# Linear attention, gated feed-forward and soft mixture of experts: the keys' maximum by 32x32 turns and partition swaps, and a new issue order

## Chip, cores and metric

One core of one Trainium2 chip. The metric is the device time of one execution in microseconds (us). TensorE (PE) multiplies, VectorE (DVE) and ScalarE (ACT) work element by element, GpSimd (POOL) does so too and issues part of the DMAs, SyncE (SP) issues the other DMAs.

## What is computed

The reference, cut to its core; all data is float32, with 8 batches, 8 heads, 576 positions and 64 features a head, so 4608 tokens of 512 features:

```python
q_s = softmax(q, axis=-1)                 # over the 64 features of a head
k_s = k - np.max(k, axis=2, keepdims=True)  # over the 576 positions
k_s = np.exp(k_s)
k_s = k_s / (np.sum(k_s, axis=2, keepdims=True) + 1e-09)
kv = np.einsum('bhsd,bhse->bhde', k_s, v)
x = np.einsum('bhsd,bhde->bhse', q_s, kv) # -> 4608 x 512
h = silu(x @ w_gate) * (x @ w_val)        # 512 -> 1536, twice
x = h @ w_out                             # 1536 -> 512
# soft mixture of experts: logits = x @ phi (32 slots); softmax over tokens feeds
# 8 experts with 4 slots each (w1: 512x1024, relu, w2: 1024x512);
# softmax over slots mixes their outputs back into each token
```

The change is about the second line: the maximum of the keys over the positions, for each of the 128 feature columns of two heads.

## The kernel before

**Tiles.** The 4608 tokens are ten blocks (eight of 512, two of 256). Attention works by batch b and by head pair p (0 to 3): a tile `kn` holds the keys of one pair, 128 partitions of positions by 128 feature columns by 5 position tiles. The gated layer works by block n and by column group i (0 to 11) in steps `pair n i`: a gate half of 12 matmuls (PSUM tile g), a value half of 12 matmuls (PSUM tile v), then Silu on ACT (L602), the product on DVE (L604, into `hT`), and for later blocks a 32x32 turn on DVE (L615) or a store. Below, "a half" is one such row of 12 matmuls of 512 columns, and halves are numbered in the order in which PE takes them.

**Keys' maximum.** `k_max(b, p)` reduces the 5 position tiles on DVE (L320, into `kpart`), turns the 128x128 result on PE (L323, `kpT`, into PSUM), and reduces it to one maximum a feature column (L326, `kmax`). `k_exp(b, p)` turns the maximum, spread over 128 columns, back on PE (L331, `kmbp`), subtracts it from the keys on DVE (L334) and takes the exponential on ACT (L338). `kv(b, p)` then multiplies with the values on PE (L346), and DVE and ACT norm the result (L352 to L355). For 8 batches of 4 pairs that is 64 turns on PE.

**Queries.** From block 2 on, `q_a` and `q_b` find maximum and sum of the queries with DVE reductions (L386, L422), four POOL copies between partition quarters (`swap`, L363), and one more DVE step (L390, L426); POOL subtracts and multiplies (L368); `q_tr` turns 32x32 blocks on DVE (L438). `x_mul` forms x on PE (L485, `px`), and ACT and DVE split it into a high and a low part (L495, L497).

**Weights.** The twelve weights W0 to W11 of the gated layer come as 64-bit numbers. Steps `w` load, `wa` (ACT, L518 and L520), `wb` (DVE, L525, L528, L532) and `wc` (POOL, L540) turn them into float32, `wh` (ACT, L553) and `wl` (DVE, L557) split them. The gate half of `pair 0 i` needs W i whole, that is after `wl i`.

**Order.** Nothing is scheduled by the compiler. The text `PROGRAM` lists steps; each mention of a step issues its next piece (up to the next `yield`), and each engine executes its instructions in that order. `@step` makes a POOL instruction wait until the named step's last DVE instruction is done. Loads of `kn`, `vn` and queries come from SP for batches 0 and 1 and from POOL after that.

**Memory.** PSUM tiles of tag m (three) are shared by `kpT`, `kmbp`, `px`, `kv` and others; g and v have two each. `kpart` has one buffer, `qst` four.

**End.** After `x 9 1`, the last step of the attention, POOL issues the loads of the expert weights (`piece`, L818), and the experts run as these land.

Of the kernel before, what the change touches and what calls it, by code (L numbers as in the profile page):

```python
# [39 lines left out]
def rows(n):  # L40
# [14 lines left out]
    vn 0 3, vn 0 2, kexp 0 3, kv 0 1, kexp 0 3, wb 3, kexp 0 2, kv 0 1, wb 3, qt 0 3, kexp 0 2, vn 0 0, w 1, kn 1 0,
    qa 1 0, wc 0@wb 3, wa 3 5, kv 0 1, kv 0 3, kv 0 0, kexp 0 2, qb 1 0, qb 0 2, kv 0 2, kv 0 0, kv 0 0, kv 0 3, wb 2,
    w 8, wa 1 3, w 4, kv 0 2, qb 1 0, qb 0 2@qa 1 0, qt 0 2, qt 0 2, x 0 0, wh 0, kv 0 3, q 1 1, kv 0 2, x 0 0, wb 2,
    wb 2, x 0 1, wl 0 v, x 0 0, x 0 0, x 0 0, kn 1 1, x 0 1, x 0 1, x 0 1, x 0 1, wb 3, qa 1 1, w 6, wc 2, wa 4 2,
    wh 2, pair 0 0, kmax 1 0, wl 2 v, wa 1 3, wc 3@qa 1 1, wb 1, pair 0 0, qb 1 0, wb 4, qb 1 1, kmax 1 0, qt 1 0,
    wh 3, const rep, wb 1, pair 0 0, wb 1, wl 3 v, w 5, wa 6 4, wc 1@wl 3 v, wa 4 2, pair 0 0, wb 4, q 1 2, pair 0 2,  # L60
    pair 0 2, kmax 1 0, qb 1 1, wh 1, wb 6, wl 1 v, pair 0 2, kmax 1 1, const rep, pair 0 3, pair 0 3, kmax 1 1, wb 6,
    vn 1 1, wb 4, w 7, wc 4@wl 1 v, pair 0 1, qb 1 1, qa 1 2, kmax 1 1, wa 5 3, kexp 1 0, qt 1 0, pair 0 2, wa 6 4,
    pair 0 3, kexp 1 1, wb 6, wc 6@wb 6, wa 7 5, wb 7, wh 4, wa 7 5, wl 4 v, kexp 1 0, wb 5, pair 0 1, pair 0 1, wh 6,
    pair 0 1, wb 5, pair 0 4, pair 0 4, kexp 1 1, wl 6 v, wa 5 3, vn 1 0, kexp 1 0, kv 1 0, wb 7, qb 1 2, kexp 1 1,
    kv 1 1, w 9 0, pair 0 3, qt 1 1, pair 0 6, wa 8 4, pair 0 6, wb 7, wa 8 4, wb 5, kv 1 1, wc 5@wb 5, qt 1 1, wb 8,
    pair 0 4, kv 1 0, wh 5, kv 1 0, pair 0 6, wb 8, wc 7@wb 8, wb 8, kn 1 2, wh 7, kmax 1 2, kmax 1 2, wl 5 v, kn 1 3,
    qb 1 2, q 1 3, pair 0 4, pair 0 3, qb 1 2, pair 0 2, wl 7 v, wa 9 5, wa 9 5, wc 8@wl 7 v, vn 1 2, vn 1 3,
    pair 0 5, pair 0 5, pair 0 5, kmax 1 3, wb 9, kmax 1 3, kv 1 1, pair 0 0, wb 9, pair 0 7, pair 0 6, kmax 1 3,
    wh 8, qa 1 3, kmax 1 2, qb 1 3, kexp 1 3, wb 9, kexp 1 3, wc 9@wb 9, w 10 1, kexp 1 2, kexp 1 2, pair 0 7, wl 8 v,
    kexp 1 3, kv 1 3, kexp 1 2, kv 1 3, wh 9, pair 0 7, kv 1 2, kv 1 2, kv 1 3, qt 1 2, wa 10 4, wl 9 v, pair 0 5,  # L70
    kv 1 2, w 11 0, wa 11 5, pair 0 8, qb 1 3, pair 0 6, wb 10, wb 10, wb 11, x 1 0, wb 10, pair 0 9, x 1 0, kn 2 0,
    wb 11, kn 2 1, q 2 1, vn 2 0, kmax 2 0, pair 0 8, pair 0 7, pair 0 7, wb 11, wa 10 4, qb 1 3, wc 10@wl 9 v, wh 10,
    pair 0 9, x 1 0, x 1 0, const phi, pair 0 8, x 1 0, o 1, wl 10 v, pair 0 8, x 1 1, qt 1 2, wa 11 5, qt 1 3,
    qt 1 3, x 1 1, x 1 1, x 1 1, x 1 1, pair 0 9, wc 11@wb 11, wh 11, wl 11 v, pair 0 10, pair 0 9, x 1 2, kmax 2 0,
    kmax 2 0, x 1 2, oa 1, pair 0 10, q 2 3, x 1 2, pair 0 11, x 1 3, pair 0 10, pair 0 10, ob 1, qa 2 1, x 1 2,
    x 1 2, qa 2 1@wl 11 v, qa 2 1, x 1 3, x 1 3, x 1 3, o 0, x 1 3, kexp 2 0, pair 0 4, oa 0, qa 2 1@qa 2 1, qb 2 1,
    qb 2 1, ob 0, pair 0 9, pair 0 11, pair 0 8, ob 1, pair 1 2, pair 1 2, ob 1, qb 2 1, oa 1, qa 2 3, pair 0 11,
    pair 1 2, kexp 2 0, kmax 2 1, pair 0 11, pair 1 2, qa 2 3, oc 1@ob 0, pair 1 4, pair 1 4, ob 0, pair 1 1,
    pair 0 10, pair 1 1, oa 0, qa 2 3, ob 0, oc 0@qa 2 3, kexp 2 0, kmax 2 1, o 2, op 0, pair 1 1, kmax 2 1, pair 1 1,
    pair 1 4, kv 2 0, op 1, op 0, qa 2 3, vn 2 1, qb 2 3, o 3, qb 2 1, oa 2, pair 1 2, qb 2 1@qb 2 1, kexp 2 1, ob 2,  # L80
    pair 1 3, oa 3, pair 1 3, qt 2 1, kn 2 3, ob 3, pair 0 1, pair 1 0, pair 1 3, pair 1 3, ob 2, pair 1 4, pair 1 0,
    pair 1 0, kexp 2 1, kv 2 0, pair 0 11, kmax 2 3, kv 2 0, ob 2, op 0, kexp 2 1, ob 3, qb 2 3, q 2 0, qa 2 0, op 1,
    kmax 2 3, pair 1 9, pair 1 1, qa 2 0, oa 3, pair 1 9, kmax 2 3, pair 1 9, qa 2 0, kv 2 1, oa 2, oc 2@qa 2 0,
    qa 2 0, pair 1 0, vn 2 2, op 0, pair 0 5, qb 2 0, qb 2 3, pair 1 9, kexp 2 3, kv 2 1, qb 2 0, pair 1 6, qb 2 0,
    pair 1 5, pair 1 5, ob 3, kn 2 2, pair 1 5, pair 1 11, qb 2 0, kexp 2 3, qb 2 0@qb 2 0, qt 2 0, pair 1 5,
    pair 1 11, q 2 2, qa 2 2, kmax 2 2, kmax 2 2, kv 2 1, kmax 2 2, pair 1 11, pair 1 11, oc 3@ob 3, qa 2 2, qa 2 2,
    x 2 0, x 2 0, kexp 2 2, kexp 2 2, pair 1 4, qa 2 2@qa 2 2, qb 2 2, qb 2 2, qb 2 2, o 5, pair 1 7, qb 2 3,
    pair 1 7, x 2 0, x 2 0, qb 2 3@qb 2 3, pair 1 6, kexp 2 3, qb 2 2, qt 2 3, pair 1 11, pair 1 7, pair 1 7,
    kexp 2 2, pair 1 7, x 2 0, pair 1 10, qb 2 2@qb 2 2, pair 1 6, kv 2 2, qt 2 2, pair 1 6, vn 2 3, q 3 0, kv 2 2,
    pair 1 0, kv 2 3, op 3, q 3 1, kv 2 3, kn 3 0, qa 3 1, vn 3 0, kv 2 2, op 1, op 1, pair 1 10, pair 1 10, qa 3 1,  # L90
    qa 3 0, qa 3 1, oa 5, kv 2 3, x 2 1, x 2 1, pair 1 10, pair 1 8, x 2 1, ob 5, op 2, x 2 1, qa 3 0, qa 3 0, x 2 1,
    vn 3 2, ob 5, pair 1 8, pair 1 8, kn 3 2, qa 3 0@qa 3 1, o 4, oa 4, oa 4, qb 3 0, pair 1 8, qb 3 0, qb 3 0@ob 5,
    pair 1 8, ob 4, ob 4, pair 2 0, pair 2 0, pair 1 5, pair 2 0, pair 2 0, op 2, qa 3 1, qb 3 1, pair 2 3, pair 2 3,
    pair 2 3, kmax 3 2, qb 3 1, pair 2 2, ob 4, oc 4, u 0, ua 0, ob 5, qb 3 1@ob 5, ub 0, pair 2 3, qb 3 0, qb 3 0,
# [1092 lines left out]
```

## Time and profile before

| | |
|---|---|
| median of 3 runs | 828.41 us (827.28 to 828.41) |
| the profiled execution, whole time | 831.53 us |
| its span | 829.8 us |
| PE busy | 781.6 us of the span |
| DVE, ACT, POOL busy | 481.7, 398.8, 261.7 us |

All rows come from one profiled execution, whose whole time is 831.53 us: 1.7 us more than its span and 3.1 us more than the median. "Busy" counts an engine's instructions; a matmul's end is modelled, so the time that a matmul takes from the next one is read from the starts of neighbours, not from its length. "Idle before" is the time in which an engine had nothing to do ahead of an instruction, with the instruction on another engine, or the DMA, that ended it.

### The profile page before, as it was taken

The numbers are of one execution on the slowest core, as the hardware profiler recorded it, in microseconds if no ns is written. First come the engines' busy times: TensorE is split into PE (matmuls) and PEld (weight loads), VectorE is DVE, ScalarE is ACT, GpSimd is POOL, SyncE is SP. The second block draws the span as 40 slices with busy tenths as digits, with TensorE's granted clock in tenths as the row PEclk, the third lists the DMA queues.
The fourth block names the chain that finished last, engine by engine and source line by source line (L and its number), as shares of the span: only waits on it lengthen the run. The fifth ranks groups of instructions, "written<-read, shape, count | busy, mean of one in ns | idle before, by whom it ended". The sixth has DMA issues, their size and how long they took to land.

```text
span 829.8 us, 15642 instructions
## 1 busy us (share of the span) xinstructions
PE 781.6 (94%) x6013; PEld 603.9 (73%) x6013; DVE 481.7 (58%) x1016; ACT 398.8 (48%) x636; POOL 261.7 (32%) x505
## 2 busy tenths in 40 slices
PE   3788999999999999999999999999999999998982
PEld 2666878877877786778777777786777788996640
DVE  7999864546565755567465666655544677144132
ACT  5978874556163562655452534333545264143032
POOL 3434343534442322322132134203132234333400
PEclk9999999999999999999999999999999999999996
DMA  9745446154245566565535573646343346999979
GB/s 359 289 147 166 149 157 211 58 212 148 100 121 151 154 148 167 128 167 160 146 80 143 141 198 76 168 140 190 92 87 100 77 117 212 297 355 398 406 286 385
DMA packets 103242, 151.08 MB, mean 182 GB/s; under 512 B 60032, under 2 KB 73728, under 8 KB 99200
## 3 DMA queue, kind: packets, MB, share of 16 engines
q1 hardware_dynamic: 86960, 90.19, 36.1%
q0 software_dynamic: 16208, 59.90, 21.1%
q8 instruction: 47, 0.77, 0.4%
q14 instruction: 27, 0.22, 0.1%
HBM read 105.22 MB, written 25.17 MB: 157 GB/s over the span
## 4 chain that ended last, share of the span: by engine, by line
PE 83%; DVE 6%; DMA 6%; ACT 2%; issue 1%; SPq 0%; POOL 0%; DVEq 0%; ACTq 0%; POOLq 0%
PE g L595 34%; PE v L595 33%; DMA piece<-in_w_dram 3%; PE lg L661 3%; PE dh L784 3%; PE px L485 2%; PE kv L346 2%; DVE W L557 1%; DMA qd<-in_qd_dram 1%; PE o L1060 1%; DMA f<-in_wgv_dram 1%; DVE ost L532 1%; DVE kn L334 1%; DVE ost L525 1%; PE qT L442 1%
## 5 line engine op out<-in xcount | busy, mean ns | idle before, releaser
L595 PE MATMUL g<-x,W 128*128 128x512 f32 (+1 forms) x1440 | 321.3, 374 | 5.5 <-DVE W L557 3.4
L595 PE MATMUL v<-x,W 128*128 128x512 f32 (+1 forms) x1440 | 316.3, 370 | 1.0 <-DVE hT L604 1.0
L595 PEld LDWEIGHTS g<-x,W 128*128 128x128 f32 x1440 | 251.8, 190 | 56.3 <-issue 4.4
L595 PEld LDWEIGHTS v<-x,W 128*128 128x128 f32 x1440 | 250.8, 189 | 50.0 <-issue 3.4
L604 DVE TENSOR_TENSOR hT<-hT,v 128x512 f32<-128x512 f32 (+1 forms) x120 | 74.6, 625 | 95.2 <-PE v L595 66.7
L602 ACT ACTIVATE hT<-g 128x512 f32<-128x512 f32 (+1 forms) x120 | 64.7, 554 | 132.5 <-PE g L595 111.7
L363 POOL COPY qsd<-qsd 32x16 f32<-32x16 f32 (+1 forms) x256 | 51.8, 202 | 195.6 <-DVE qsd L386 101.1
L368 POOL TENSOR_TENSOR qd<-qd,qsd 128x512 f32<-128x512 f32 (+1 forms) x64 | 59.9, 939 | 85.8 <-DVE qsd L390 40.1
L602 ACT ACT_TABLE_LOAD x56 | 71.8, 1283 | 22.2 <-PE g L595 7.2
L615 DVE STREAM_TRANSPOSE hB<-hT 128x512 f32<-128x512 f32 (+1 forms) x78 | 50.8, 671 | 1.0 <-DMA hN<-hB 0.2
L495 ACT ACTIVATE x<-px 128x512 fp32r<-128x512 f32 (+1 forms) x44 | 21.6, 516 | 46.5 <-PE px L485 34.2
L818 POOL DMA_DIRECT2D piece<-in_w_dram x54 | 28.5, 531 | 44.7 <-PE v L595 21.5
L334 DVE TENSOR_TENSOR kn<-kn,kmbp 128x640 f32<-128x640 f32 x32 | 25.7, 809 | 20.8 <-PE kmbp L331 20.8
L540 POOL TENSOR_TENSOR ost<-ost,f 128x1024 int32<-128x1024 int32 x9 | 23.2, 2581 | 40.9 <-DVE ost L532 11.0
L292 POOL DMA_DIRECT2D kn<-in_kn_dram x24 | 13.9, 578 | 68.2 <-PE kv L346 57.5
L338 ACT ACT_TABLE_LOAD x16 | 20.5, 1283 | 30.1 <-DVE kn L334 29.6
L338 ACT ACTIVATE kn<-kn 128x640 f32<-128x640 f32 x32 | 23.2, 736 | 23.2 <-DVE kn L334 23.1
L497 DVE TENSOR_TENSOR x<-px,x 128x512 fp32r<-128x512 f32 (+1 forms) x44 | 24.7, 577 | 13.3 <-ACT x L495 12.1
L326 DVE TENSOR_REDUCE kmax<-kpT 128x1 f32<-128x128 f32 x32 | 9.1, 285 | 40.0 <-PE kpT L323 39.9
L346 PEld LDWEIGHTS kv<-vn,kn 128*32 128x32 f32 x1280 | 23.8, 149 | 9.9 <-issue 3.8
L540 POOL TENSOR_TENSOR ost<-ost 128x1024 int32<-128x1024 int32 x9 | 22.9, 2544 | 21.4 <-DVE ost L532 8.9
L320 DVE TENSOR_REDUCE kpart<-kn 128x128 f32<-128x640 f32 x32 | 25.8, 806 | 6.6 <-DMA kn<-in_kn_dram 6.5
(175 smaller groups left out, 883.4 us busy)
## 6 DMA issues: line engine op xcount, KB each, us to landing
piece<-in_w_dram POOLq DMA_DIRECT2D x54, 512.0 KB, 8.0
hN<-hB SPq DMA_DIRECT2D x400, 48.0 KB, 2.2
f<-in_wgv_dram SPq DMA_DIRECT2D x9, 1024.0 KB, 9.4
vn<-in_vn_dram POOLq DMA_DIRECT2D x24, 325.0 KB, 4.5
kn<-in_kn_dram POOLq DMA_DIRECT2D x24, 320.0 KB, 4.1
out_dram<-ob SPq DMA_DIRECT2D x7, 1024.0 KB, 9.9
hT_dr<-hT SPq DMA_DIRECT2D x24, 256.0 KB, 5.4
qd<-in_qd_dram POOLq DMA_DIRECT2D x24, 256.0 KB, 4.5
```

The lines of the kernel that those rows point to most:

```text
L320: nc.vector.tensor_reduce(out=part, in_=kn_t[b, p], axis=AX, op=ALU.max)
L334: nc.vector.tensor_tensor(out=t, in0=t, in1=mb.unsqueeze(2).to_broadcast([128, 128, ST]), op=ALU.subtract)
L338: nc.scalar.activation(out=t, in_=t, func=ACTF.Exp)
L346: nc.tensor.matmul(acc[r:r + 32, :], lhsT=ek[:, r:r + 32, i], rhs=vv[:, i, r // D, :], start=(i == 0), stop=(i == ST - 1), tile_position=( ...
L363: nc.gpsimd.tensor_copy(out=st[a:a + 32, o + 1], in_=st[b:b + 32, o])
L368: nc.gpsimd.tensor_tensor(out=a, in0=a, in1=s, op=op)
L540: nc.gpsimd.tensor_tensor(out=d, in0=d, in1=t[:, c, 0], op=ALU.add)
L595: nc.tensor.matmul(gv[j], lhsT=W[i][:, w, k, j, :], rhs=x[:, k, :], start=(k == 0 and w == 0 and x is xh), stop=(k == KT - 1 and w == 1),)
L602: nc.scalar.activation(out=s, in_=g, func=ACTF.Silu)
L604: nc.vector.tensor_tensor(out=s, in0=s, in1=v, op=ALU.mult)
L615: nc.vector.transpose(out=hB[n, i // w][:, :, i % w, :], in_=s.rearrange("p (b j) -> p b j", j=32))
L818: nc.gpsimd.dma_start(out=ap, in_=src)
```

## The change

For batches 1 to 7 the keys' maximum goes another way, for two head pairs at once. `k_part` (`kr`) does the first reduction as before, into one half of a tile. `k_all` (`km`) then does: a 32x32 turn in place on DVE (128x256), a reduction to 128x8 on DVE, four POOL copies that swap neighbouring partition quarters, a maximum on DVE, four POOL copies that swap halves, a maximum on DVE, and a 32x32 turn of the spread result into one PSUM tile (128x256), from which `k_exp` subtracts. Batch 0 keeps its PE turns. Some small tiles share buffers with others. The whole of `PROGRAM` is laid out anew; it has as many steps as before (2301).

```diff
+    def k_part(b, p):
+        if len(kpart.get(b, ())) == 0:
+            kpart[b] = [sm.tile([128, 2, 128], F32, tag="kpart", bufs=1, name="kpart")]
+        nc.vector.tensor_reduce(out=kpart[b][0][:, len(kpart[b]) - 1], in_=kn_t[b, p], axis=AX, op=ALU.max)
+        kpart[b].append(p)
+
+    def k_all(b, h):
+        part, *ps_ = kpart.pop(b)
+        t = part.rearrange("p j (b i) -> p (j b) i", i=32)
+        nc.vector.transpose(out=t, in_=t)
+        st = sm.tile([128, 2, H], F32, tag="qst", bufs=4, name="kst")
+        o = st[:, 0]
+        nc.vector.tensor_reduce(out=o, in_=t, axis=AX, op=ALU.max)
+        yield
+        for x in (1, 2):
+            swap(st, 0, x)
+            yield
+            nc.vector.tensor_tensor(out=o, in0=o, in1=st[:, 1], op=ALU.max)
+            yield
+        mb = misc((128, 2, 128), "kmb")
+        nc.vector.transpose(
+            out=mb.rearrange("p j (b i) -> p (j b) i", i=32), in_=o.unsqueeze(2).to_broadcast([128, 8, 32])
+        )
+        for j, p in enumerate(ps_):
+            kmax[b, p] = mb[:, j]
+
     def k_exp(b, p):
-        mx, mb = kmax.pop((b, p)), misc((128, 128), "kmbp")
-        nc.tensor.transpose(mb, mx.to_broadcast([128, 128]), ident)
-        yield
+        mb = kmax.pop((b, p))
+        if not b:
+            mx, mb = mb, misc((128, 128), "kmbp")
+            nc.tensor.transpose(mb, mx.to_broadcast([128, 128]), ident)
+            yield
         t = kn_t[b, p]
...
-    def swap(st, o):
+    def swap(st, o, x=1):
 
         for g in range(4):
-            a, b = 32 * g, 32 * (g ^ 1)
+            a, b = 32 * g, 32 * (g ^ x)
             nc.gpsimd.tensor_copy(out=st[a:a + 32, o + 1], in_=st[b:b + 32, o])
```

Four lines of the new order, from the stretch in which the weights W1 to W4 are made ready, and `kr` and `km` of batch 1 stand among them:

```diff
+    x 0 1, x 0 1, pair 0 0, wc 3@qa 1 1, wh 2, wl 2 v, wh 3, pair 0 0, wa 6 4, w 4, wb 1, wl 3 v, q 1 2, wb 6, kr 1 1,
+    kr 1 0, km 1 0, qb 1 1, wa 4 2, wb 4, vn 1 1, pair 0 0, vn 1 0, w 9 0, qt 1 0, wc 1@wl 3 v, qb 1 1, wh 1, wb 6,
+    wb 4, km 1 0, wb 4, w 7, km 1 0, pair 0 2, pair 0 2, pair 0 2, qb 1 1, w 8, wl 1 v, pair 0 3, wa 4 2, qt 1 1,
+    wb 6, pair 0 1, km 1 0, wc 4@wl 1 v, qa 1 2, wa 6 4, pair 0 1, qt 1 0, wc 6@wb 6, wa 5 3, kn 1 2, wa 7 5, km 1 0,
```

## Rows read from the trace of the kernel before

**Rows 1.** The page: span, and each engine's busy time.
```profile
span 829.8 us, 15642 instructions
PE 781.6 (94%) x6013; PEld 603.9 (73%) x6013; DVE 481.7 (58%) x1016; ACT 398.8 (48%) x636; POOL 261.7 (32%) x505
```

**Rows 2.** Three stretches: length, busy us (instructions) by engine, PE clock, DMA share, GB/s.
```profile
0.00:92.34 92.34, 69.16 (x620) 54.03 (x621) 83.49 (x120) 73.12 (x159) 34.87 (x23) 0.96 0.60 218
92.34:690.00 597.66, 594.09 (x4063) 460.08 (x4062) 350.33 (x757) 289.32 (x395) 187.78 (x414) 1.00 0.50 139
690.00:829.80 139.80, 118.32 (x1335) 89.83 (x1334) 47.85 (x141) 36.32 (x84) 39.03 (x70) 0.95 0.91 341
```

**Rows 3.** What PE waited for from 92.34 to 690: us, times, longest.
```profile
PE px L485 <- DVE wp L580: 2.1, 1, 2.1
PE v L595 <- DVE hT L604: 0.8, 1, 0.8
PE kv L346 <- ACT kn L338: 0.7, 3, 0.3
```

**Rows 4.** PE in order of time: start, length, instruction; turns alone between halves.
```profile
349.46 2.89 PE L595 MATMUL v<-x,W 128*128 128x512 f32 x12
352.19 0.27 PE L323 MATMUL kpT<-ident,kpart 128*128 128x128 f32 x1
352.21 3.00 PE L595 MATMUL g<-x,W 128*128 128x512 f32 x12
355.05 0.27 PE L331 MATMUL kmbp<-ident,kmax 128*128 128x128 f32 x1
355.07 3.01 PE L595 MATMUL v<-x,W 128*128 128x512 f32 x12
357.92 2.88 PE L595 MATMUL g<-x,W 128*128 128x512 f32 x12
360.64 0.62 PE L595 MATMUL v<-x,W 128*128 128x512 f32 x2
```

**Rows 5.** PE in order of time: turns beside other work between halves.
```profile
167.99 0.27 PE L323 MATMUL kpT<-ident,kpart 128*128 128x128 f32 x1
168.19 1.09 PE L485 MATMUL px<-qsT,kvs 64*64 64x128 f32 x16
169.21 0.32 PE L331 MATMUL kmbp<-ident,kmax 128*128 128x128 f32 x1
169.29 3.00 PE L595 MATMUL g<-x,W 128*128 128x512 f32 x12
```

**Rows 6.** Groups by line and shape: busy us, mean ns of one, idle before.
```profile
L323 PE MATMUL kpT<-ident,kpart 128*128 128x128 f32 x32 | 9.8, 308 | 10.5 <-DMA ident<-in_ident_dram 6.6 <-DVE kpart L320 3.9
L326 DVE TENSOR_REDUCE kmax<-kpT 128x1 f32<-128x128 f32 x32 | 9.1, 285 | 40.0 <-PE kpT L323 39.9
L438 DVE STREAM_TRANSPOSE qsT<-qd 128x256 f32<-128x256 f32 x8 | 3.5, 442 | 3.8 <-POOL qd L368 2.9 <-PE px L485 0.9
L386 DVE TENSOR_REDUCE qsd<-qd 128x8 f32<-128x256 f32 x8 | 3.2, 396 | 2.5 <-DMA qd<-in_qe_dram 2.5
L390 DVE TENSOR_TENSOR qsd<-qsd 128x8 f32<-128x8 f32 x8 | 1.2, 145 | 0.3 <-POOL qsd L363 0.3
L363 POOL COPY qsd<-qsd 32x8 f32<-32x8 f32 x64 | 11.8, 185 | 44.8 <-DVE qsd L422 21.5 <-DVE qsd L386 21.3
```

**Rows 7.** What DVE waited for, whole span: us, times, longest.
```profile
DVE kn L334 <- PE kmbp L331: 20.8, 11, 3.4
DVE qsd L426 <- POOL qsd L363: 7.8, 10, 1.0
DVE qsd L390 <- POOL qsd L363: 5.3, 7, 2.2
```

**Rows 8.** PE in order of time, in the start; idle before it in brackets.
```profile
33.38 4.60 PE L595 MATMUL g<-x,W 128*128 128x512 f32 x12 [2.10 <-DVE x L497]
77.87 4.15 PE L595 MATMUL g<-x,W 128*128 128x512 f32 x10 [1.75 <-DVE W L557]
92.34 0.95 PE L595 MATMUL g<-x,W 128*128 128x512 f32 x3
```

**Rows 9.** DVE in order of time, in the start.
```profile
43.70 1.22 DVE L557 TENSOR_TENSOR W<-ost,W 128x1024 fp32r<-128x1024 f32 x1
44.83 0.68 DVE L604 TENSOR_TENSOR hT<-hT,v 128x512 f32<-128x512 f32 x1
45.43 2.57 DVE L528 TENSOR_SCALAR ost<-ost 128x1024 int32<-128x1024 int32 x1
...
89.24 1.74 DVE L557 TENSOR_TENSOR W<-ost,W 128x1024 fp32r<-128x1024 f32 x1
```

**Rows 10.** POOL in order of time, in the start.
```profile
44.99 2.45 POOL L540 TENSOR_TENSOR ost<-ost,f 128x1024 int32<-128x1024 int32 x1 [5.37 <-DVE W L557]
```

More of the change, by code (lines that the diff above doesn't have):

```diff
@@ L55 @@
[L55 to L94, printed above, removed]
@@ new lines @@
+    pair 0 6, km 1 1, wb 9, pair 0 7, wh 8, wb 9, qt 1 2, qa 1 3, vn 1 3, kv 1 1, km 1 1, const phi, km 1 1, wb 9,
+    km 1 1, kexp 1 3, pair 0 5, pair 0 5, kexp 1 2, q 2 1, wa 9 5, pair 0 7, kexp 1 3, pair 0 5, kv 1 3, wl 8 v,
+    kv 1 3, w 10 1, wc 9@wb 9, kexp 1 2, vn 2 0, pair 0 4, kv 1 2, kn 2 1, kv 1 2, qb 1 3, kv 1 2, wh 9, wl 9 v,
+    pair 0 6, wa 10 4, wb 10, wb 10, pair 0 8, kv 1 3, wa 10 4, qb 1 3, wb 10, pair 0 8, qa 2 1, x 1 0, pair 0 7,
+    pair 0 9, kn 2 0, pair 0 8, pair 0 8, x 1 0, pair 0 9, x 1 0, wc 10@wl 9 v, w 11 0, wa 11 5, wb 11, wb 11,
@@ new lines @@
+    qb 4 2, pb 2, qa 4 1, lt 0 0, ts 0 0, ts 0 0, ts 0 0, qb 4 1, ud 2, ts 0 0, pair 3 2, pair 3 2, pair 3 2,
+    pair 3 7, sh 2 2, sh 2 2, ts 0 0, pair 3 1, ts 0 0, kn 4 2, kr 4 2, pb 2, qb 4 2, pb 2, kv 4 3, kn 4 1, ts 0 0,
+    ts 0 0, pc 2, pair 3 1, qb 4 1, qb 4 1, lt 0 1, vn 4 1, pair 3 1, pair 3 2, qb 4 1, qb 4 1, qt 4 1, pair 3 0,
+    pair 3 1, pb 2, pb 2, q 4 3, vn 4 2, lg 3 0, kr 4 1, qb 4 2, pair 3 5, pair 3 10, pair 3 10, km 4 1, km 4 1,
+    km 4 1, pair 3 4, km 4 1, pair 3 10, qb 4 2, pair 3 4, pc 2, km 4 1, km 4 1, kv 4 3, kv 4 3, kexp 4 1, kn 5 1,
@@ new lines @@
+    kv 5 2, kv 5 2, kexp 5 3, sh 4 0, kv 5 3, kv 5 3, kv 5 2, q 6 0, kn 6 0, kn 6 1, kv 5 3, lg 4 1, x 5 1, x 5 1,
+    x 5 1, pair 4 11, pair 4 11, pair 4 11, pair 4 8, sh 4 1, sh 4 1, qa 6 0, kr 6 1, x 5 1, x 5 1, qa 6 0, qa 6 0,
+    pair 4 9, vn 6 1, qa 6 0, qb 6 0, pair 5 3, pair 5 1, pair 5 1, pair 4 8, pair 4 7, pair 4 11, kr 6 0, lt 1 0,
+    pair 5 3, pair 4 6, qa 6 1, qa 6 1, pair 5 2, qb 6 0, pair 4 9, qa 6 1, qa 6 1, qb 6 1, pair 5 3, qb 6 1,
+    pair 5 1, pair 4 10, lg 4 2, qb 6 0, lg 1 0, pair 4 11, km 6 0, sh 4 2, sh 4 2, pb 3, pair 4 9, pair 5 0,
@@ new lines @@
+    kv 7 1, x 7 0, km 7 1, pc 1, qb 7 3, km 7 1, qb 7 3, qt 7 3, q 8 1, pair 6 5, qb 7 2, pair 6 5, pair 6 11,
+    pair 6 11, pc 5, qb 7 2, x 7 0, vn 7 3, pair 6 9, pd 4, pair 6 9, pair 6 5, pair 6 11, x 7 0, km 7 1, qa 8 1,
+    qa 8 1, kexp 7 2, pair 6 4, qt 7 2, qa 8 1, kexp 7 3, kexp 7 3, pair 6 10, q 8 0, qa 8 1, qb 8 1, pair 6 10,
+    kexp 7 2, qb 8 1, pair 6 10, kv 7 2, kv 7 3, lg 6 1, kv 7 2, sh 6 0, sh 6 0, qb 8 1, kv 7 3, kv 7 2, kv 7 3,
+    x 7 1, sh 6 1, pair 6 10, qb 8 1, sh 6 1, pair 6 8, pair 6 8, sh 6 1, pair 6 6, x 7 0, x 7 1, pair 6 7, qb 8 1,
@@ L942, in exp_table @@
     def exp_table(_=0):
-        t = sm.tile([128, 1], F32, tag="one", name="one")
+        t = sm.tile([128, 1], F32, tag="krs", name="one")
         nc.scalar.activation(out=t, in_=ident[:, 0:1], func=ACTF.Exp)
     def u_rz():
-        rz = keep["rz"] = sm.tile([128, 1], F32, tag="rz", name="rz")
+        rz = keep["rz"] = sm.tile([128, 1], F32, tag="krs", name="rz")
         nc.vector.tensor_scalar_add(rz, Z, EPS)
```

288 lines of the change are left out of this document (153 added, 135 removed).

## The prediction

> **What bounds the kernel now.** I read the busy times first, then the three stretches, then what PE waits for. PE is busy for 781.6 of 829.8 us [rows 1], but the 48 us that it is idle are not spread evenly. In the middle stretch, 92.34 to 690 us, PE is busy for 594.1 of 597.7 us at full clock, with DVE at 59% and POOL at 31% [rows 2]. Its idle time of 3.6 us there is one wait of 2.1 us and four small ones [rows 3]. So the middle is bound by the sum of PE's work: what PE no longer does there comes off the time, unless a wait takes its place. In the start, 0 to 92.34, DVE is busy for 83.5 us and PE for only 69.2 [rows 2]: PE gets its halves as fast as DVE makes the weights ready. Twice a half comes after a wait on DVE and then runs slowly (4.60 us against a spacing of 2.7) [rows 4, 8]. In the end, from 690, the DMAs are 91% busy at 341 GB/s [rows 2]; the expert weights flow there, their loads begin after the last attention step, and the order from that step on is nearly the same text. An earlier middle moves the end forward as a whole, so I cost the end at nothing. If DMA bandwidth were taken by something moved into it, that cover would be gone; no load of keys, values or queries is left by then.
>
> **PE: the turns that go.** For batches 1 to 7, 28 head pairs lose two turns each, 56 of 64. Eight of these stand ahead of the half that first uses W8, where PE follows DVE; they are counted at nothing. 48 stand in the middle stretch. What one is worth is read from neighbouring starts. Two halves in a row start 2.72 us apart (357.92 to 360.64) [rows 4]. With a `kpT` between them, 352.19 to 355.05 is 2.86, so 0.14 us for the turn; with a `kmbp`, 355.05 to 357.92 is 2.87, so 0.15. Beside other work a turn at the head of a group holds the next step for 0.20 us (167.99 to 168.19), and one at its tail for 0.08 (169.21 to 169.29) [rows 5]. Counted in the old text, the 48 are 17 in groups of their own (9 alone, 4 times two) at 0.145, which makes 2.5 us, and 31 beside other work at 0.13, near the middle of 0.08 and 0.20, as heads and tails of groups are about equally many: 4.0. Sum 6.5 us; with all 31 at 0.08 or at 0.20 it is 5.0 or 8.7.
>
> The instruction itself is listed at 308 ns in the mean and 0.27 us in the middle stretch [rows 4, 6], most of it beside the next instruction; taken whole, 48 x 0.27 would be 13.0 us. The Trainium skill ("TensorE: Matmul & The Clock Gate", Part 4: PE-mode transpose) gives about 275 ns for a 128x128 turn in one kernel's context; by that figure 13.2 us would stand here instead of 6.5. The listed length agrees with the page, the spacing of the starts doesn't, and the sum goes by the spacing.
>
> **PE: the regrouping.** Counted in the two texts behind the first W8 half, the old order leaves the halves 60 times for other work, 13 of them for turns alone; that leaves 47, against 41 in the new order. A break costs about what a lone turn does, 0.13 us: 6 x 0.13 = 0.8 us, with bounds 0 and 1.5. Of ACT's table loads, the new text asks for 106 changes between Silu and Exp instead of 112, on an engine that is half idle [rows 1]: nothing.
>
> **DVE.** For each set of two pairs two reductions at 0.285 go (0.57 us). In come a turn of 128x256 (0.44), a reduction to 128x8 (0.40), two maxima (0.145 each) and a turn into PSUM, for which no row stands; its bounds are the 128x256 turn at 0.44 and twice that, and I take 0.44 [rows 6]. That is 1.57, so 1.0 us more a set and 14 us in all; DVE goes from 482 to about 496 us. Twelve sets lie in the middle, where DVE is idle for 247 us [rows 2]. It also loses its waits on PE's turns, 39.9 and 20.8 us [rows 6, 7]. On POOL 14 x 8 copies at 0.185 make 20.7 us, beside 410 idle us in the middle [rows 2, 6]. ACT keeps its work.
>
> **The added wait.** DVE now waits twice a set for four POOL copies. Behind it on DVE stand the products that free PE's value tile; PE has two of these, so a wait shorter than a pair (5.4 us) stays hidden. The same hop exists for the queries, 64 times, and cost DVE 7.8 + 5.3 us in 17 waits, at most 2.2 [rows 7]: about 0.2 a hop, 28 hops, 6 us of idle DVE. On POOL the copies stand among key loads and query steps, which come later by up to 0.74 a hop; with both in order, a load stuck on a busy buffer would hold DVE too. PSUM tiles of tag m are asked for 42 times less, which only loosens. For the waits of PE in the middle I keep today's 3.6 us, a change of 0, with bounds -3.6 (all go) and +7 (0.5 us a set).
>
> **The start.** Here the sets of batch 1 and the new order meet the engine that binds. I summed DVE's work by the rows' durations up to the last step that a weight needs. Up to `wl 5` both orders have 61.2 us; up to `wl 8` the old has 71.8 and the new 74.2: two sets (+2.0) and one more product (+0.7), less a cast moved. Now W8 is ready at 90.98 (89.24 + 1.74) and its half starts at 92.34 [rows 8, 9], so 1.4 of the 2.5 are covered and PE waits 1.1 us more. Against that stand the holds. When POOL runs a weight step of 2.45 us, a DVE instruction that comes beside it can be held to its end: 2.57 us at 45.43 where 0.68 is usual, until POOL's 44.99 + 2.45 [rows 9, 10]. POOL has nine weight steps (L540) before 92.34, of which one stands in the rows. In the new text `wc 1` runs beside `kr`, `kr` and the first turn of `km`, which may give the 1.9 us of this hold back. I take +1.1, with bounds -4 (two holds gone) and +12 (below). The loads of W0, W2, W3 and W1 keep their order on SP; those of W4 to W9 change places, behind DMAs that are 60% busy over the start [rows 2], and I cost them at nothing. If one came late, its W would wait by the time of a load.
>
> **Sum.** -6.5 - 0.8 + 0 + 1.1 = -6.2 us on the profiled 831.5, so 825.3 there. The profiled time stands 3.1 above the median of 828.4, so the forecast is 822.2 us.
>
> **Rivals.** (A) The whole length: if a turn costs PE its listed 0.27 us, 828.4 - 13.0 - 0.8 + 1.1 = 815.7. For it speaks the list, against it the spacing between halves. The page cited above would have it so. Chance 0.10.
>
> (B) The hop takes the gain: each of the 14 sets holds PE by 0.5 us, because in an order packed this tightly DVE's wait for POOL falls where a half waits for its tile: 822.2 + 7 = 829.2, no change. For it speaks that several `kv` steps follow closely on the set that feeds them (`kv 4 1` with no half between), against it that PE waited for keys' exponentials only 0.7 us in the whole middle [rows 3]. Chance 0.20.
>
> (C) Slower: the holds in the start. The two maxima of a set read two SBUF inputs, as the weight subtraction does that was held. If each of batch 1's four maxima comes beside a weight step of POOL and is held to its end, DVE is late by 4 x 2.4 = 9.6 us in the one stretch where it binds, and PE, idle longer, takes one more half at the slow rate (+1.9, 4.60 against 2.72) [rows 4, 8]: 822.2 + 9.6 + 1.9 = 833.7. It decides the sign once the start loses more than the 7.3 us that PE gains. For it speaks `wc 6`, issued right ahead of the second maximum of the first set; against it, that holds are there in the old order too, so only additional ones count. The Trainium skill ("GPSIMD Engine Reference", 8. Key points) says that POOL shares its SBUF interfaces with DVE, in contention with DVE instructions that have two SBUF inputs or a two-port mode; the held rows agree. Chance 0.18.
>
> (D) The turns beside other work were free, because PE lost that time to the change of shape anyway, so the change takes away less than it says: 2.5 + 0.8 off, 828.4 - 3.3 + 1.1 = 826.2. For it speaks that a half after a `px` or a turn is late by nearly the same [rows 5]. Chance 0.10, just faster.
>
> The forecast itself has 0.42. Faster by over 0.2% (under 826.8; 0.2% is about what a measurement of this kernel can tell from no change) collects 0.42 + 0.10 and most of (D): 0.60. Within 0.2%: 0.22, that is (B) and the rest of (D). Slower: 0.18. The range must leave out no more than 2 in 10: from 815, which takes in (A), to 831.5, which takes in (B) and the lighter half of (C). The forecast's own range is 818 to 826.
>
> **What would show it.** Right: PE has 56 instructions less (5957) and L323 and L331 stand at 8 turns in all; PE's idle time in the middle stays at 2 to 6 us while that stretch is 5 to 9 us shorter; the half that first uses W8 starts at 92 to 95 us; DVE stands near 496 us and POOL near 282. (A) would show as a middle shorter by 12 us or more; (B) as waits of PE for DVE behind the copies; (C) as held DVE instructions in the start and a W8 half after 100 us. The prediction fails if the new order moves work that I did not sum (ACT's table loads, query steps) in front of a half, or if the end starts later than the middle allows, which would show as the last attention step not moving forward with the halves.

## The result and the profile after

The changed kernel takes 816.02 us, the median of four runs (815.42 to 816.83), against 828.41 for the kernel before, measured beside it. The ratio is 0.9837, with a 95% interval of 0.9812 to 0.9862. The gain is 12.4 us, twice the forecast 6.2. The profiled execution of after took 816.83 us (span 815.1), 0.8 above its median, where that of before stood 3.1 above its own. So the two spans differ by 14.7 us, and that is the number that the stretches below have to add up to. In the later rounds of runs the kernel before had medians of 830.28 to 830.89 us (eight to ten runs each), so the 828.41 of this round stands low, and 12.4 is rather the lower end of the gain. In one kernel below (the new middle behind the old start) one execution of six took 1968.21 us; it is left out of that kernel's median and ratio.

The page of after, span and busy times (it answers to [rows 1]):

```profile
span 815.1 us, 15636 instructions
PE 771.2 (95%) x5957; PEld 594.6 (73%) x5957; DVE 481.0 (59%) x1058; ACT 390.2 (48%) x630; POOL 288.8 (35%) x617
```

PE lost 56 instructions and 10.4 us of busy time, and DVE's total did not rise. To see where the time went, the span is cut at two places that can be found in both kernels: the start of the 17th half, the first that needs W8 (92.34 us before [rows 8], 83.76 after), and the start of the 204th half. First the three stretches of after (columns as in [rows 2]):

```profile
0.00:83.76 83.76, 63.88 (x612) 50.93 (x612) 73.56 (x122) 69.30 (x148) 42.37 (x40) 0.98 0.65 248
83.76:673.15 589.39, 588.83 (x4015) 454.88 (x4009) 359.82 (x796) 280.76 (x397) 205.80 (x506) 1.00 0.51 140
673.15:815.10 141.95, 118.47 (x1339) 88.84 (x1337) 47.61 (x143) 40.10 (x88) 40.59 (x72) 0.95 0.89 336
```

Then the same two later stretches of before, from the same halves:

```profile
92.34:689.56 597.22, 593.65 (x4059) 459.64 (x4058) 349.89 (x756) 288.88 (x395) 187.35 (x413) 1.00 0.50 139
689.56:829.80 140.24, 118.76 (x1339) 90.27 (x1337) 48.29 (x142) 36.76 (x84) 39.46 (x70) 0.95 0.90 340
```

The start is 8.6 us shorter (92.34 to 83.76), the middle 7.8 (597.22 to 589.39), and the end 1.7 longer. In the middle PE's busy time fell by 4.8 us and its idle time by 3.0. What is left of the idle time is two waits. PE's waits in the middle of after (us in total, times, longest):

```profile
PE lrep L724 <- DVE llo L706: 0.4, 1, 0.4
PE v L622 <- DVE hT L631: 0.2, 1, 0.2
```

The new way itself, by groups (busy us, mean ns of one | idle before), in after:

```profile
L320 PE MATMUL kpT<-ident,kpart 128*128 128x128 f32 x4 | 1.9, 467 | 10.8 <-DMA ident<-in_ident_dram 6.5 <-DVE kpart L317 4.3
L390 POOL COPY kst<-kst 32x8 f32<-32x8 f32 x112 | 27.6, 247 | 62.2 <-DVE kst L340 45.5 <-DVE kst L345 12.2
L345 DVE TENSOR_TENSOR kst<-kst 128x8 f32<-128x8 f32 x28 | 5.9, 210 | 7.2 <-POOL kst L390 7.1
L348 DVE STREAM_TRANSPOSE kmb<-kst 128x256 f32<-128x256 f32 x14 | 6.3, 450 | 0.2
```

Only batch 0's four `kpT` are left. The turn into PSUM, for which no row stood, takes 450 ns (0.44 was taken). DVE waited 7.1 us for the copies in 28 hops, against the 6 expected. The copies took 27.6 us where 20.7 were taken. So the parts of the change cost what was forecast, or not much more; the difference lies elsewhere, above all in the start.

### The profile page after: what moved, and what is told of

Same layout as the page of the kernel before. It is cut to its first block, busy times and chain, and to the rows that moved or that the text cites. A ratio compares the mean times of both kernels' runs of the same rounds, so it can differ in the third digit from the quotient of the medians.

```text
span 815.1 us, 15636 instructions
## 1 busy us (share of the span) xinstructions
PE 771.2 (95%) x5957; PEld 594.6 (73%) x5957; DVE 481.0 (59%) x1058; ACT 390.2 (48%) x630; POOL 288.8 (35%) x617
## 4 chain that ended last, share of the span: by engine, by line
PE 85%; DMA 7%; DVE 4%; ACT 2%; issue 1%; SPq 0%; DVEq 0%; POOLq 0%
PE v L622 35%; PE g L622 34%; DMA piece<-in_w_dram 4%; PE dh L811 3%; PE kv L373 3%; PE lg L688 3%; PE px L512 2%; DMA vn<-in_vn_dram 1%; PE o L1087 1%; DMA h0T<-hT_dr 1%; DVE W L584 1%; DMA q<-in_q_dram 0%; PE hNp L668 0%; DVE ost L559 0%; PE h L1023 0%
## 5 line engine op out<-in xcount | busy, mean ns | idle before, releaser
L622 PE MATMUL g<-x,W 128*128 128x512 f32 (+1 forms) x1440 | 318.1, 372 | 1.3 <-DVE x L524 1.3
L395 POOL TENSOR_TENSOR qd<-qd,qsd 128x512 f32<-128x512 f32 (+1 forms) x64 | 61.6, 968 | 69.3 <-DVE qsd L454 32.5
L390 POOL COPY kst<-kst 32x8 f32<-32x8 f32 x112 | 27.6, 247 | 62.2 <-DVE kst L340 45.5
L449 DVE TENSOR_REDUCE qsd<-qd 128x16 f32<-128x512 f32 (+1 forms) x32 | 19.4, 607 | 17.4 <-ACT qd L446 17.3
L446 ACT ACTIVATE qd<-qd 128x512 f32<-128x512 f32 (+1 forms) x32 | 18.4, 577 | 23.5 <-POOL qd L395 23.3
L373 PE MATMUL kv<-vn,kn 128*32 128x65 f32 x1280 | 26.6, 238 | 2.9 <-ACT kn L365 1.9
L413 DVE TENSOR_REDUCE qsd<-qd 128x16 f32<-128x512 f32 (+1 forms) x32 | 19.3, 605 | 16.7 <-DMA qd<-in_qd_dram 8.5
```

The costliest lines, as they stand in the source:

```text
L373: nc.tensor.matmul(acc[r:r + 32, :], lhsT=ek[:, r:r + 32, i], rhs=vv[:, i, r // D, :], start=(i == 0), stop=(i == ST - 1), tile_position=( ...
L390: nc.gpsimd.tensor_copy(out=st[a:a + 32, o + 1], in_=st[b:b + 32, o])
L395: nc.gpsimd.tensor_tensor(out=a, in0=a, in1=s, op=op)
L622: nc.tensor.matmul(gv[j], lhsT=W[i][:, w, k, j, :], rhs=x[:, k, :], start=(k == 0 and w == 0 and x is xh), stop=(k == KT - 1 and w == 1),)
```

## Where the start went: instructions of DVE that POOL holds

Three groups of DVE carry most of it. They prepare and split the weights; the view is that of the groups by line and shape from 0 to 83 us, first before, then after:

```profile
L557 DVE TENSOR_TENSOR W<-ost,W 128x1024 fp32r<-128x1024 f32 x8 | 17.3, 2160 | 0.3 <-ACT W L553 0.3
L525 DVE TENSOR_SCALAR ost<-ost 128x1024 f32<-128x1024 f32 x10 | 10.6, 1068 | 1.2 <-ACT ost L518 1.2
L528 DVE TENSOR_SCALAR ost<-ost 128x1024 int32<-128x1024 int32 x10 | 8.7, 866 | 0.0
```

```profile
L584 DVE TENSOR_TENSOR W<-ost,W 128x1024 fp32r<-128x1024 f32 x9 | 13.1, 1455 | 0.6 <-ACT W L580 0.6
L552 DVE TENSOR_SCALAR ost<-ost 128x1024 f32<-128x1024 f32 x10 | 7.4, 735 | 1.7 <-ACT ost L545 1.7
L555 DVE TENSOR_SCALAR ost<-ost 128x1024 int32<-128x1024 int32 x10 | 6.7, 684 | 0.1
```

It is the same work on the same shapes, but a `wl` takes 2160 ns in the mean before and 1455 after, where an undisturbed one takes 1.22 us [rows 9]. I summed, over all single DVE instructions before 92 us, what each takes beyond the usual time of its form, where that is over 0.25 us: 17.2 us before, 4.8 after. Below, such an excess beside a step of POOL is called a hold. The forecast knew one of them, of 1.9 us.

What one does to PE is seen at W4 in the trace of before (start, length, instruction; POOL, DVE and PE in order of time):

```profile
57.46 2.74 POOL L540 TENSOR_TENSOR ost<-ost,f 128x1024 int32<-128x1024 int32 x1 [2.08 <-DVE ost L532]
...
57.85 3.43 DVE L557 TENSOR_TENSOR W<-ost,W 128x1024 fp32r<-128x1024 f32 x1
...
59.12 0.61 PE L595 MATMUL g<-x,W 128*128 128x512 f32 x2
61.34 0.96 PE L595 MATMUL g<-x,W 128*128 128x512 f32 x3 [1.61 <-DVE W L557]
```

POOL's weight step ends at 60.20. The `wl` beside it ends at 61.28, 1.08 us later, about its own usual length: it did its work after POOL's step, not beside it. PE had taken the two matmuls that need W4's high part alone, and stood for 1.61 us until the low part came. W5 went the same way (its `wl` took 2.69 us from 75.12, and PE waited the 1.75 us of [rows 8]), and after that second stall the clock was granted at half, 1.2 GHz, from 78.3 to 81.7 us, which is why that half took 4.15 us for ten matmuls. After shows neither stall nor that fall; its one fall, from 32.6 to 36.0 us, stands in its first half, as one of before's does. The Trainium skill ("Trainium Architecture — The Big Picture", What this means for kernel authors) says that the port pair of DVE and GpSimd is an exclusive lock and not a split of bandwidth; the 1.08 us agree with that.

What DVE runs beside a step of POOL in the new order, in after, again in order of time, the POOL row first:

```profile
40.21 2.82 POOL L567 TENSOR_TENSOR ost<-ost,f 128x1024 int32<-128x1024 int32 x1 [3.44 <-DVE W L584]
```

```profile
40.65 1.54 DVE L331 TENSOR_REDUCE kpart<-kn 128x128 f32<-128x640 f32 x2
42.22 0.45 DVE L337 STREAM_TRANSPOSE kpart<-kpart 128x256 f32<-128x256 f32 x1
42.70 0.42 DVE L340 TENSOR_REDUCE kst<-kpart 128x8 f32<-128x256 f32 x1
43.04 0.68 DVE L552 TENSOR_SCALAR ost<-ost 128x1024 f32<-128x1024 f32 x1
```

`kr` twice, the turn and the reduction of `km` fill POOL's 40.21 to 43.03, and each takes its usual time; the next `wb` step, of a form that is held elsewhere, begins as POOL ends. That is the stretch named in the prediction as one that "may give the 1.9 us of this hold back".

## The experiments

### POOL's weight steps cut to 8 of 1024 columns, in both kernels

Theory: the holds cost the start its time. Rival: the new text is shorter there for another reason (fewer waits on PE's turns, another order of the weights).

```diff
     def cv_c(key, c=FULL):
         t = f64_t[key] if c[1] < 1024 else f64_t.pop(key)
-        c = slice(*c)
+        c = slice(*c) if key[0] != "w" else slice(c[0], c[0] + 8)
```

Of before:

> The kernel before, with POOL's addition in the step that completes each weight made over 8 of 1024 columns (the low bits of W are left out in the rest, so the values are slightly off). Orders and waits stay. If the old start is long because POOL's 2.45 us steps hold DVE (17.2 us of excess before 92 us), the first W8 half comes 8 to 14 us earlier and the whole time falls by about that. If the start is bound by DVE's own work and by data, it comes 0 to 3 us earlier.

Of after:

> The same cut of POOL's addition in the changed kernel, whose excess before 92 us is 4.8 us. If holds make the difference between the two starts, the two cut kernels reach the first W8 half within 2 us of each other, and this one gains only 2 to 5 us on the changed kernel. If something else in the new start makes it short, the two cut kernels still differ by 6 us or more there.

Before so cut takes 820.22 us, a ratio of 0.9883 (0.9859 to 0.9906); after so cut 814.81, 0.9818 (0.9796 to 0.9840). The 17th half (order of time, start first), of before cut, then of after cut:

```profile
82.29 3.00 PE L595 MATMUL g<-x,W 128*128 128x512 f32 x12
```

```profile
82.44 3.18 PE L622 MATMUL g<-x,W 128*128 128x512 f32 x12
```

With the holds gone the old start gains 10.05 us (92.34 to 82.29), the new one 1.3, and the two starts are equal within 0.15 us. The 1.3 is hardly more than repeats differ by: two later runs whose start has the text of after, uncut, reach the 17th half at 84.52 and 84.87. The holds themselves fell from 17.2 us to 0.8 in the cut kernel before, as its `wl` group shows (0 to 83 us):

```profile
L557 DVE TENSOR_TENSOR W<-ost,W 128x1024 fp32r<-128x1024 f32 x10 | 12.2, 1220 | 2.8 <-ACT W L553 2.8
```

The cut also takes away POOL's own 2.45 us in each weight's chain, and that is a rival for the 10. If DVE had stood waiting for those chains, its idle time would fall with them. The start of before so cut, up to its 17th half (columns as in [rows 2]):

```profile
0.00:82.29 82.29, 64.69 (x621) 51.88 (x621) 68.04 (x121) 72.03 (x159) 12.43 (x23) 1.00 0.69 255
```

DVE is busy for 15.45 us less than in before (68.04 against 83.49) and idle for 5.4 more (14.25 against 8.85). So it is busy time that went, not waiting. The clock's column is 1.00: both stretches at the lower clock are gone with the stalls, and what they cost is part of the 10.05. The middle stayed: 596.3 us before so cut, against 597.2.

### Each half of the change alone: new start, old middle, and the reverse

Theory: start and middle gain apart from one another, and add up. Rival: the middle's gain comes from the earlier start, or the start's from the turns that go.

```diff
 PROGRAM = """
...
-    x 1 1, x 1 1, x 1 1, q 2 3, kr 2 1, qb 1 3, qt 1 3, pair 0 10, wh 11, x 1 0, pair 0 9, pair 0 9, wl 11 v,
+    x 1 1, x 1 1, x 1 1, q 2 3, qb 1 3, qt 1 3, pair 0 10, wh 11, x 1 0, pair 0 9, pair 0 9, wl 11 v, const rep,
...
-        if not b:
+        if (b, p) in turned:
```

New order and new way for batch 1, then the old order and PE's turns from batch 2 on:

> The new order and the new way up to the 23rd half (batch 1's keys among it), and behind that the old order with PE's turns for batches 2 to 7. If the start gives most of the unforeseen gain by itself, as the starts of the halves in the two traces say (the first half that uses W8 starts 8.6 us earlier), this is 7 to 9 us below the kernel before. If those 8.6 us were slack that the old middle takes back, it is less than 3 us below it.

The old order and PE's turns up to the same place, then the new ones:

> The old order with PE's turns for batch 1 up to the same place, and behind it the new order and the new way for batches 2 to 7. If the middle is worth what the traces show between the W8 half and the last attention step (7.8 us, of which 3 are waits that went), this is 5 to 8 us below the kernel before, and with the new start it adds up to the whole gain. By my sum for the turns and the regrouping alone it is 7.3 below. If the whole length of a turn counts, it is 13 below.

The same kernel once more, for its profile:

> The old start and the new middle again, for its profile. The first W8 half should start near 92 us, as in the kernel before, and the stretch from there to the last attention step should be 6 to 9 us shorter than in the kernel before, so that the whole time is 5 to 8 us below it.

The new start alone gives 824.18 us, 0.9934 (0.9911 to 0.9956), 6.2 below the 830.42 of the kernel before beside it, a little less than the 7 to 9 expected; the new middle alone 824.52, 0.9925 (0.9896 to 0.9954), and again 824.30, 0.9928 (0.9899 to 0.9958), which is 5.9 and 6.6 below. The 17th half with the new start and with the old one:

```profile
84.52 3.04 PE L630 MATMUL g<-x,W 128*128 128x512 f32 x12
```

```profile
92.54 2.99 PE L628 MATMUL g<-x,W 128*128 128x512 f32 x12
```

And the middle of the kernel with the old start, up to its 204th half:

```profile
92.54:680.86 588.32, 588.15 (x4011) 455.17 (x4010) 360.74 (x792) 277.51 (x385) 207.65 (x507) 1.00 0.51 142
```

That middle is 8.9 us shorter than before's, with an old start; the new start is 7.8 shorter, and its old middle measures 598.1, as before. The profiled spans fall by 6.1 and 8.4, together 14.5 of the 14.7. Two separate gains, then, and the one that the forecast had the wrong way round is the start's.

### The order alone, and the way alone

Which of the two makes the start shorter: the new instructions or the new order? First the new order with PE's turns put back, two to a set in each direction:

```diff
-        t = part.rearrange("p j (b i) -> p (j b) i", i=32)
-        nc.vector.transpose(out=t, in_=t)
...
+        t = misc((128, 2, 128), "kpT")
+        for j in range(2):
+            nc.tensor.transpose(t[:, j], part[:, j], ident)
...
+        for j in range(2):
+            nc.tensor.transpose(mb[:, j], mx[:, j:j + 1].to_broadcast([128, 128]), ident)
```

> The new order, but batches 1 to 7 take the keys' maximum with PE's turns again, two pairs at a time at the places of the new steps; the 32x32 turns and the swaps are gone. My forecast blamed the way (the turns) for nearly all of the gain and nothing on the order of the start. If the order brought the start's 8.6 us by fewer held DVE instructions, the first W8 half still starts near 84 us and the time is 5 to 9 us above the changed kernel (56 turns at 0.13 to 0.15 us). If DVE's and POOL's new instructions are what keeps the holds away, the start falls back by 4 us or more, and the time is 10 or more above the changed kernel. If a turn costs its whole 0.27 us, it is 15 above.

It takes 861.37 us, 1.0359 (1.0331 to 1.0387), far beyond the 5 to 9, or 10 or more, over the changed kernel that were expected. PE's waits say why (whole span):

```profile
PE v L620 <- DVE hT L629: 11.4, 6, 4.4
...
PE kv L371 <- ACT kn L363: 5.9, 3, 2.4
```

The order puts a set's steps where DVE and POOL do them without PE. With turns in them DVE stands until PE comes to the turn, behind it stand the products that free the value tiles, and PE waits for these; the trace also shows six more falls of the clock to its lower level than that of after, up to 607 us. Its 17th half comes at 89.21, 5.4 us later than in after, which was to show that the new instructions keep the holds away. But the holds in its start are 3.6 us, as few as in after; DVE is idle there for 19.4 us instead of 10.2. So the order removes the holds, what comes late does so by waiting, and the time as a whole can't be compared with a forecast for turns.

Then the old order with the new way, one pair at a time (224 copies, twice as many as in the change):

```diff
+        if b:
+            t = part.rearrange("p (b i) -> p b i", i=32)
+            nc.vector.transpose(out=t, in_=t)
...
+            swap(st, 0, 1)
+            yield
+            nc.vector.tensor_tensor(out=o, in0=o, in1=st[:, 1], op=ALU.max)
+            swap(st, 0, 2)
```

> The kernel before, in its old order, with the keys' maximum of batches 1 to 7 by 32x32 turns and swaps, one pair at a time at the places of the old steps (224 POOL copies of 32x4). If the order is what shortened the start, the first W8 half starts at 92 us or later here, with some 17 us of holds as before, and the whole time lies between 8 us below and 4 us above the kernel before: the turns' 6 to 7 us less whatever the 84 hops cost, of which those in the start count in full. If the way itself keeps the holds away, the W8 half starts at 88 us or earlier.

851.46 us, 1.0257 (1.0236 to 1.0278). The holds in its start are 17.3 us, as before, and the 17th half starts at 95.21. Over the whole span DVE and PE wait in turn (first DVE's row, then PE's):

```profile
DVE kst L330 <- POOL kst L384: 16.9, 17, 3.0
```

```profile
PE kv L367 <- ACT kn L359: 8.3, 6, 4.2
```

In the forms tried here, neither the way nor the order gains alone. This is much like rival (B), in an order not laid out for the hop and with twice the copies.

### The hop: each swap twice

Forecast: POOL's copies and DVE's wait are hidden. Rival (B): the hop takes the gain.

```diff
         for x in (1, 2):
+            swap(st, 0, x)
             swap(st, 0, x)
```

> The changed kernel with each group of four POOL copies of the keys made twice, so that every one of the 28 hops that DVE waits for is about 0.75 us longer. If the added wait is hidden, as I forecast for the middle, the time rises by 0 to 2 us. If the new order needs each hop on time (rival B), it rises by up to 28 x 0.75 = 21 us, and by 5 or more in any case.

825.49 us, 0.9930 (0.9902 to 0.9958): 9.5 us over the 816.02 of after, 8.3 by the spans, for 112 copies more, which at 0.185 us each [rows 6] are 20.7. The start pays 3.9 of it (the 17th half at 87.61), the middle 3.8. DVE's and PE's waits, whole span:

```profile
DVE kst L346 <- POOL kst L391: 24.5, 20, 2.0
```

```profile
PE kv L374 <- ACT kn L366: 5.2, 3, 1.9
```

So the hop of the change itself is hidden (0.6 us of waits in the whole middle), but there is little cover left: a hop twice as long shows for nearly half.

### What a turn costs PE

The term of 6.5 us had three places: alone between halves, ahead of other work, behind it. Each run below adds turns of the constant identity to after, whose result nobody reads. First, one in each `kr` and one in each `kexp` of batches 1 to 7, 56 in all, into a tile of its own:

```diff
+        nc.tensor.transpose(misc((128, 128), "more"), ident, ident)
```

> The changed kernel with 56 more PE turns of the identity, one at each first reduction and one ahead of each subtraction of batches 1 to 7, on whose result nothing waits. It measures the disputed price by itself: 5 to 9 us more at 0.10 to 0.16 us for each, 15 us more at the whole length of 0.27.

852.0 us, 1.0245 (1.0214 to 1.0276), 36 us over after, which fits neither price. The waits in the middle show what it measured:

```profile
PE more L333 <- DVE x L527: 4.4, 1, 4.4
PE more L362 <- DVE qsd L420: 4.1, 1, 4.1
```

Six such waits hold 19.7 us, and four falls of the clock come on top: PE waits for a PSUM tile of tag m, not for the turn. The run says nothing on the turn's price; it says what asking for 56 more of these tiles can cost in this order. The next two write into tiles that are there anyway.

Alone between halves, 56 of them, ahead of value halves:

```diff
+                if 1 <= n < 8 and i < 8:
+                    nc.tensor.transpose(gv[1][:, 0:128], ident, ident)
```

> The changed kernel with 56 more PE turns, each straight ahead of the value half of a pair (blocks 1 to 7, weights 0 to 7) and into that half's own PSUM tile, so that no further tile is asked for and nothing waits on it. Against the run with 56 turns into tiles of their own this takes the wait for a PSUM tile away. At the price read from neighbouring starts (0.14 to 0.15 us alone) it is 8 us above the changed kernel; at the whole length 15; if the price was mostly the wait for a tile, it is 8 or less here against the 36 measured there.

824.14 us, 0.9925 (0.9909 to 0.9940): 8.1 over after, 0.145 us a turn; by the spans 7.3, 0.13; from the 17th to the 204th half, where all 56 stand, 7.9, 0.14. In order of time, and the group's listed length:

```profile
311.55 2.88 PE L624 MATMUL g<-x,W 128*128 128x512 f32 x12
314.28 0.27 PE L621 MATMUL v<-ident 128*128 128x128 f32 x1
314.30 3.00 PE L624 MATMUL v<-x,W 128*128 128x512 f32 x12
```

```profile
L621 PE MATMUL v<-ident 128*128 128x128 f32 x56 | 15.4, 275 | 0.0
```

The list says 275 ns; PE loses half of that. The Trainium skill ("TensorE: Matmul & The Clock Gate", Part 4: PE-mode transpose) gives about 275 ns for such a turn in one kernel's context, and the listed length agrees with it. The first matmul behind the turn starts only 0.02 us after it, and the 0.14 shows in the matmuls that follow. So the distance from a turn's start to the next start is not its price.

Ahead of other work, 44 of them (28 ahead of `kv`, 16 ahead of `x`):

```diff
-        acc = misc((128, D + 1), "kv")
+        acc = misc((128, 128), "kv")
+        if b:
+            nc.tensor.transpose(acc, ident, ident)
+        acc = acc[:, 0:D + 1]
...
+            nc.tensor.transpose(px[0][:, 0:128], ident, ident)
```

> The kernel after, with 44 more PE turns of the constant identity that nobody reads, each at the head of a group of other work between halves: one ahead of the products of every kv step of batches 1 to 7 (28) and one ahead of the first product of every x step from block 2 on (16), into the tile that the step writes anyway, so that no new PSUM tile is asked for. This is the disputed term by itself: what a turn costs PE beside other work. If it is the forecast's 0.13 us (between 0.08 and 0.20), the time rises by 5.7 us (3.5 to 8.8) over the kernel after. If turns beside other work are nearly free (rival D, and what the middle's own saving of 4.8 us instead of 7.3 asks for, 0.05 us a turn), it rises by 0 to 2.2. If such a turn costs its listed 0.27 us, by 12.

825.93 us, 0.9943 (0.9923 to 0.9963): 9.9 over after. From the 17th to the 204th half the trace is 9.16 us longer (598.55 against 589.39), with 39 of the turns there; the waits don't grow (0.6 us in all, as in after). In order of time, the same place in after, then with two of the turns:

```profile
162.89 5.60 PE L622 MATMUL v<-x,W 128*128 128x512 f32 x24
168.42 1.49 PE L373 MATMUL kv<-vn,kn 128*32 128x65 f32 x80
169.71 0.63 PE L593 MATMUL wpT<-ost,phi_sb 128*32 128x256 f32 x8
```

```profile
165.42 5.61 PE L626 MATMUL v<-x,W 128*128 128x512 f32 x24
170.86 0.27 PE L372 MATMUL kv<-ident 128*128 128x128 f32 x1
171.06 0.86 PE L376 MATMUL kv<-vn,kn 128*32 128x65 f32 x40
171.86 0.33 PE L372 MATMUL kv<-ident 128*128 128x128 f32 x1
172.12 0.87 PE L376 MATMUL kv<-vn,kn 128*32 128x65 f32 x40
172.78 0.64 PE L597 MATMUL wpT<-ost,phi_sb 128*32 128x256 f32 x8
```

From the value halves to `wpT` it is 6.82 us without and 7.36 with the two turns: 0.54 more. The first gives 0.11 of it: `kv` starts 5.53 us after the halves without it and 5.64 with it. The second, between two `kv` steps, gives the other 0.43.

The price depends on the neighbours. To take it over the whole stretch, I measured from the last matmul ahead of a turn to the seventh matmul behind it, and compared that with the same two neighbours without a turn. Behind a half and ahead of `kv` or `px` a turn costs 0.135 us in the mean (18 turns), between small work and `px` 0.24 (11 turns), between small work and `kv` 0.42 (10 turns). The sum is 9.3, against the 9.16 of the trace. Rival (D), free turns beside other work, doesn't hold at these places; how it fares where the old turns stood follows below.

### Fewer, larger copies

The second swap moves whole halves, so two copies of 64 partitions can do it instead of four of 32. That takes 28 copies from POOL:

```diff
+        if x == 2:
+            for a in (0, 64):
+                nc.gpsimd.tensor_copy(out=st[a:a + 64, o + 1], in_=st[64 - a:128 - a, o])
+            return
```

> The changed kernel with the second swap of each set as two copies of 64 partitions instead of four of 32, so 14 hops are shorter by about 0.37 us. Doubling every group cost 9.5 us for 28 hops of 0.75; if the hops' cost goes on downward in the same way, this gains 14 x 0.37 x 0.45 = 2.3 us on the changed kernel; if only the two sets in the start count, 0.7; if a 64-partition copy takes as long as two of 32, nothing.

815.84 us, 0.9826 (0.9811 to 0.9842): no difference from after that the intervals would show. The hops did get shorter: a copy of 64 partitions takes 188 ns in the median, one of 32 takes 185, and DVE's wait for the copies fell from 7.1 to 5.2 us. So what went was hidden already.

## Why the prediction was off

**The start is the step that failed.** Its term was +1.1 us, with bounds -4 and +12, and it came out at -8.6. The extra work was right in kind: up to `wl 8` DVE does more. But the prediction summed DVE's work "by the rows' durations", counted of the holds "only additional ones", because they "are there in the old order too", priced one by [rows 9, 10], and bounded the gain at "two holds gone" (-4). "Nine weight steps" (the trace has ten), "of which one stands in the rows", was the hint to follow: summed over the start the holds were 17.2 us, and 12.4 of these went. Not all of that reaches PE, since W8's path had 1.4 us of slack and some holds fall on work that nothing waits for. The cut kernel before shows how much does: 10.05 us. The stalls and both stretches of half clock are gone in that kernel too. The prediction had read the two waits of [rows 8] as the pace of DVE's work, and ahead of each stands a held `wl` step:

```profile
29.45 3.27 DVE L557 TENSOR_TENSOR W<-ost,W 128x1024 fp32r<-128x1024 f32 x1 [0.33 <-ACT W L553]
75.12 2.69 DVE L557 TENSOR_TENSOR W<-ost,W 128x1024 fp32r<-128x1024 f32 x1
```

The first fall of the clock decides little: after has it too, and two runs with after's start don't (the 84.52 and 84.87 above), and they are no faster there.

The measured 816.0 lies above the 815 at which the stated range begins, but that bound was drawn to take in (A), which didn't hold: it is luck that the time lies inside.

**The middle's sum was right by luck: its errors cancel.** Forecast -7.3, measured -7.8. The waits, taken as unchanged, fell from 3.6 to 0.6 us, close to the bound -3.6; which step of the new order took away the one of 2.1 us at `px` [rows 3] was not followed. PE's work fell by 4.8 instead of 7.3, and most of that error lies in the turns. The prediction read those beside other work by the distance from a turn's start to the next start (0.20 and 0.08 in [rows 5]), which is not their price. Measured as above, the 48 turns in before's middle cost some 4.9 us instead of 6.5: nine alone 0.14 each and four pairs 0.24 a pair (2.2 us together, 2.5 forecast), 16 that stood last in a group 0.06 each and 15 that stood first 0.12 (2.7 together, 4.0 forecast). That leaves about nothing for the regrouping, priced at -0.8; it is a remainder and was not measured by itself. The price of 0.145 alone is confirmed.

**The hop** was right: hidden in the middle, 7.1 us of idle DVE against 6 expected. **POOL** stands at 288.8 us instead of 282, because a copy takes 247 ns in the mean and not 185; the excess, 6.9 us over 112 copies, is the whole difference, and those in the start are the long ones (422 ns in the mean). **DVE** was to rise to 496 us and stayed at 481.0. Its groups that came and went differ by 16.2 us (14 forecast), and 12.4 of the 16.9 that went elsewhere are the holds of the start; the other 4.5 were not traced one by one.

**The end**, taken at nothing, came out 1.7 us longer. The order there is the same text in both kernels but for its first steps, some 20 of 400. Of the runs with after's order in the middle that stretch took from 139.4 us (turns into tiles of their own) to 142.6 (swaps twice), around before's 140.2. Whether the 1.7 are the kernel's or the run's stays open.

**The rivals.** (A), 0.27 us a turn, would have left a middle shorter by 12 us or more. (B) doesn't hold for the change, but for its way in the old order. (C) had the right mechanism with the wrong sign: weight steps of POOL holding DVE in the start did decide, but the new order had fewer of them, and the four maxima that stand in the start are held little (160 ns in the mean, 145 for their like in [rows 6]). (D) was right in part: beside other work the old turns were not free, but cost two thirds of what was forecast (2.7 us instead of 4.0).

## What to carry to other kernels

Where one engine holds another's instructions, sum the excess over the usual length across the whole stretch that this engine binds, before pricing what an order adds to it: one row shows the mechanism, not its size. A new order can be worth as much as the instructions that it removes, and neither need gain without the other. The price of a small PE instruction is how much later the work behind it comes than between the same neighbours without it: neither its listed length, nor the distance from its start to the next.
